# Reordering the attention and first routing stage of a fused attention and two-MoE kernel: loads, fillers, ranks, early products

## The chip, the cores and the metric

The kernel runs on one core of a Trainium2 chip. The metric is the device time of one execution in microseconds (us), lower is better; 485.15 us is the median of three runs of the kernel before (485.13 to 485.38). The engines are named as in the profile: PE (TensorE; PEld is its weight load), DVE (VectorE), ACT (ScalarE), POOL (GpSimd) and SP (SyncE, which here only issues DMAs). Each engine works through its own instructions in order; they wait for one another by semaphores.

## The reference

Three stages follow one another on 2304 tokens (4 batches of 576) of 512 features (8 heads of 64).

```
kv  = einsum('bhsd,bhse->bhde', k, v);  out = einsum('bhsd,bhde->bhse', q, kv)   # linear attention
x   = out / sqrt(mean(out*out, -1) + 1e-6) * g_norm                  # per head
MoE 1:  tokens with x @ w_skip > 0 go to expert argmax(x @ w_gate) of 8:
        x += p_max * (relu(x @ w1[e]) @ w2[e])                       # others pass unchanged
MoE 2:  every token goes to its argmax expert, at most `capacity` tokens per expert (in token order):
        out = p_max * (relu(x @ w1[e]) @ w2[e]), zero for tokens beyond it
```

All inputs and outputs are float32. Which token goes to which expert is known only at run time, so the experts' batches are built on the chip.

## The kernel before, in words

Tokens are worked on as 18 tiles of 128. Everything that this case turns on lies in the first 78 us of 484.

**Attention stage.** SP loads k and v of the four batches (`load_kv`, into the shared weight buffers `wraw`) and q, transposed on the way in as `qT` (`load_q`). Per batch, `emit_kv` multiplies v by k in five chunks c0 to c4 of the sequence, ACT copies the result to `vk`, and `emit_kvT` multiplies it by the gate weights and transposes it; ACT copies both into `kvbd`. Per tile, `emit_products` multiplies q by `kvbd` (one 128x162 product for each of four head pairs: 128 outputs and 34 router logits) into one of three `ops` tiles of PSUM. `emit_tile` then squares on ACT, sums on DVE (`ss`), takes the root on ACT and the reciprocal on DVE (`ri`), scales the logits on DVE (`lh`, then a reduction into `xa`); the outputs go by an ACT copy to `xa`, where POOL multiplies them by the gain `au` and then by `ri`. A finished tile of `xa` is stored by SP to the DRAM table `xcat`.

**Routing.** `rank_part1` makes a one-hot expert matrix `oh` (DVE), counts and ranks by products with ones and triangles (PE, letter R), and builds for each tile a comparison matrix `As` (DVE), which PE multiplies by `Bt` into a table of token numbers by expert (letters E for tiles 0 to 8, T for tiles 9 to 17). It runs twice. The first pass covers tiles 0 to 8: it finds the expert with most tokens (`lead1`), a register is loaded with its number (`order_1l`), SP loads its weights, and POOL gathers its first 128 tokens from `xcat`. These 128 tokens are slot 0's early rows; their transposes (letter q), first-layer products h0 to h3 (`l1`) and second-layer products y0 to y3 (`l2`) are PE work that needs no second pass. The second pass covers tiles 9 to 17 after the last tile. `sort_experts` orders the experts by count, `by_slot` sorts the table into slots, and `rests` sums what exceeds the slots' capacities to one number `nrest`. All engines load `nrest` and branch on it (`If(nrest > 0)`); for these inputs the branch is not taken, but nothing behind it starts before. Behind it stands the rest of MoE 1 and all of MoE 2, beginning with `t1`, PE transposes of gathered rows.

**What sets the order.** PE's order is written by hand: `ATT_SEQ` has one string per batch (t = a tile, c = a chunk of the next batch's k-v product, T = `emit_kvT`, r/R = a rank pass on DVE / on PE, e/E = register / early table, m = products alone, g = gain alone, s = store, w = one weight load, f = fillers, q, h as above), and `EARLY_SEQ` what follows the attention. `WARM_0`, `WARM_T`, `WARM_E` are counts of filler products (of zeros, nobody reads them) on PE. The other engines are ordered by a scheduler, with `behind(a, b)` to keep a behind b.

Of the kernel before, what the change touches and what calls it, by code (L numbers as in the profile page):

```python
# [18 lines left out]
T = B * S  # L19
# [21 lines left out]
WARM_E = 12  # L41
# [7 lines left out]
def moe_kernel(ctx: ExitStack, tc: tile.TileContext, qT, kk, vv, aux, w1a, w2a, w1b, w2b, capacity, out):  # L49
# [68 lines left out]
    cap_i = cst.tile([128, 2], I32, name="cap_i")  # L118
    nc.scalar.dma_start(out=cap_i, in_=capacity.bitcast(I32).unsqueeze(0).to_broadcast([128, 2]))
    capf = cst.tile([128, 1], F32, name="capf")  # L120
# [93 lines left out]
    def rank_part1(st, i0, i1, bump=None):  # L214
# [33 lines left out]
        if prev is not None:  # L248
            counts()
            key = rt.tile([128, E], F32, name="key_1")  # L250
            nc.vector.tensor_tensor(out=key, in0=cps, in1=st["head"], op=ALU.add)
            cnt0 = rt.tile([1, E], F32, name="cnt0_1")
            after = nc.vector.tensor_copy(out=cnt0, in_=cps[0:1])
            st.update(ends=cnt0)
            sort_experts(st, key)
# [13 lines left out]
        row, lead = (lg[:, 256:384], lead1(lg, cps, ranked, st)) if prev is None else (rowb, iter(()))  # L269
# [25 lines left out]
    def lead1_rest(lg, cps, st):  # L295

        order, key, mx = st["lead"]
        lack, oneP = (lg[:, c:c + E] for c in (228, 236))
        one = rt.tile([128, E], F32, name="lead_1l")
        nc.vector.tensor_scalar(out=one, in0=key, scalar1=mx, scalar2=None, op0=ALU.is_equal)  # L300
        nc.vector.tensor_scalar(out=oneP, in0=key, scalar1=mx, scalar2=None, op0=ALU.is_equal)
# [5 lines left out]
        st["lead"] = order, one, bump, head  # L307
# [23 lines left out]
    def sort_experts(st, key):  # L331
# [3 lines left out]
        v.tensor_tensor(out=G, in0=key.unsqueeze(1).to_broadcast([128, E, E]),  # L335
                        in1=key.unsqueeze(2).to_broadcast([128, E, E]), op=ALU.is_gt)
# [109 lines left out]
    def overflow(m, r, w1, w2, gcol0, limit, add_tokens):  # L446
# [4 lines left out]
        with tc.If(nrest > 0):  # L451
            with tc.tile_pool(name=nm("ov"), bufs=1) as ov, tc.tile_pool(name=nm("ovp"), bufs=1, space=PSUM) as ovp:
# [214 lines left out]
    def l1(j, fp, c0=0, c1=None, early=False):  # L667
# [4 lines left out]
        hp = p1h.tile([128, 2, c1 - c0], F32, name="hp1")  # L672
        for ff in range(2):
            fc = fp * 2 + ff
            wv = W[j][fc // 4].rearrange("p (f k m) -> p f k m", f=4, k=4)
            for k in range(4):
                nc.tensor.matmul(hp[:, ff, :], lhsT=wv[:, fc % 4, k, :], rhs=XT[j][:, k, c0:c1], start=(k == 0), stop=(k == 3))  # L677
        if j in SPLIT1:
# [43 lines left out]
    with att:  # L722
        warm(p1u.tile([128, 512], F32, name="acc"), 10)
# [34 lines left out]
        for b in range(B):  # L758
            load_kv(b)
            load_q(b)  # L760
# [24 lines left out]
        def emit_kvT(b):  # L785

            vk, kb = vk_all[b % 2], kvbd_all[b % 2]
            if b == B - 1:
                spare.append(apo.tile([128, 4, 256], F32, name="ops").rearrange("p c n -> p (c n)"))
                tp = spare[0][:, 0:512].rearrange("p (c n) -> p c n", c=4)  # L790
# [3 lines left out]
            wp = p1u.tile([128, 4, 128], F32, name="acc")  # L794
# [37 lines left out]
        def emit_gain(i):  # L832

            gained.add(i)
# [4 lines left out]
            else:  # L839
                nc.scalar.copy(out=og4, in_=o4)  # L840
                multiply(og, og, grep.unsqueeze(1))

        def emit_tile(i):
# [9 lines left out]
            if i not in gained:  # L853
                emit_gain(i)
# [13 lines left out]
        with tc.manual_schedule(engines={mybir.EngineType.PE}):  # L868
            emit_kv(0, range(5))
            emit_kvT(0)  # L870
            def early1():

                order, one, bump, r1["head"] = r1["lead"]
                ahead["reg"] = slot_reg(order, 0, False)
                W[0] = []
                return one, bump

            def early1_rows(n, one):
# [3 lines left out]
                for i in range(n):  # L882
# [650 lines left out]
```

## Time and profile before

| | |
|---|---|
| median of 3 runs | 485.15 us |
| profiled execution, device time | 485.83 us |
| its span (first to last instruction) | 484.1 us |
| PE busy | 470.4 us, 97% of the span |
| DVE, ACT, POOL busy | 298.8, 203.6, 145.3 us |
| moved by DMA | 104.90 MB in 23641 packets |

A line of the timeline gives the start in us from the beginning of the span, the length in us, engine, source line of the kernel before, operation, tiles written and read, shapes and the count of instructions merged into the line; in brackets the idle time of the engine just before it and what released it. The profiled execution lies 1.73 us above its own span; that part is outside the first and last instruction. PE is the busiest engine by far, but its gaps are not spread evenly: most lie in the first 78 us.

### The profile page before, as it was taken

The numbers are of one execution on the slowest core, as the hardware profiler recorded it, in microseconds if no ns is written. First come the engines' busy times: TensorE is split into PE (matmuls) and PEld (weight loads), VectorE is DVE, ScalarE is ACT, GpSimd is POOL, SyncE is SP. The second block draws the span as 40 slices with busy tenths as digits, with TensorE's granted clock in tenths as the row PEclk, the third lists the DMA queues.
The fourth block names the chain that finished last, engine by engine and source line by source line (L and its number), as shares of the span: only waits on it lengthen the run. The fifth ranks groups of instructions, "written<-read, shape, count | busy, mean of one in ns | idle before, by whom it ended". The sixth has DMA issues, their size and how long they took to land.

```text
span 484.1 us, 10279 instructions
## 1 busy us (share of the span) xinstructions
PE 470.4 (97%) x3852; PEld 444.6 (92%) x3852; DVE 298.8 (62%) x950; ACT 203.6 (42%) x507; POOL 145.3 (30%) x179
## 2 busy tenths in 40 slices
PE   8999989999999999999899999999999999999995
PEld 3788788999999999999798999999999999999985
DVE  2367786676676755448694664756747656776611
ACT  1575542545353331225142553554545544555400
POOL 5586865022213113111243220401506033040201
PEclk9999999999999999999999999999999999999999
DMA  7999967997876955566039964554755566310001
GB/s 264 396 395 351 326 227 256 323 367 288 289 238 219 329 195 195 173 231 247 24 94 413 391 259 168 201 189 129 248 176 191 185 229 213 110 38 1 36 24 40
DMA packets 23641, 104.90 MB, mean 217 GB/s; under 512 B 3529, under 2 KB 3657, under 8 KB 14880
## 3 DMA queue, kind: packets, MB, share of 16 engines
q1 hardware_dynamic: 16144, 76.70, 44.6%
q0 software_dynamic: 7152, 27.40, 16.2%
q8 instruction: 32, 0.52, 0.4%
q14 instruction: 25, 0.20, 0.1%
q10 hardware_dynamic: 288, 0.07, 0.1%
HBM read 92.15 MB, written 12.76 MB: 217 GB/s over the span
## 4 chain that ended last, share of the span: by engine, by line
PE 74%; DVE 5%; DMA 3%; issue 1%; ACT 0%; POOL 0%; POOLq 0%; ACTq 0%
PE hp L677 13%; PE yp L1197 8%; PE yp L1198 8%; PE yp L1199 8%; PE hp L1197 6%; PE yp L701 6%; PE hp L1198 6%; PE hp L1199 6%; PE yp L711 3%; PE yp L702 2%; PE yt L1426 2%; PE tp L1382 2%; DMA wraw<-in_w2b 1%; DVE wlo L1087 1%; PE tp L659 1%; PE tp L1118 1%
## 5 line engine op out<-in xcount | busy, mean ns | idle before, releaser
L1086 ACT CAST whi<-wraw 128x512 fp32r<-128x512 f32 x152 | 86.3, 621 | 75.2 <-PE yp L1198 30.1
L1087 DVE TENSOR_TENSOR wlo<-wraw,whi 128x512 fp32r<-128x512 f32 x152 | 97.4, 684 | 28.9 <-ACT whi L1086 27.7
L416 POOL DMA_INDIRECT rows<-xcat,gi x40 | 42.6, 1064 | 149.0 <-ACT ex L425 87.8
L1197 PE MATMUL hp<-xh,whi 128*128 128x256 f32 (+7 forms) x256 | 78.9, 308 | 0.3 <-DVE hl L1217 0.2
L1199 PE MATMUL hp<-xh,wlo 128*128 128x256 f32 (+7 forms) x256 | 76.7, 299 | 0.0
L1198 PE MATMUL hp<-xl,whi 128*128 128x256 f32 (+7 forms) x256 | 76.6, 299 | 0.0
L677 PE MATMUL hp<-xT,wraw 128*128 128x140 f32 (+8 forms) x560 | 75.6, 291 | 0.5 <-ACT xT L661 0.5
L677 PEld LDWEIGHTS hp<-xT,wraw 128*128 128x128 f32 x560 | 71.6, 190 | 2.6 <-issue 1.8
L1197 PE MATMUL yp<-hh,whi 128*128 128x320 f32 (+5 forms) x192 | 58.8, 306 | 0.0
L1416 POOL DMA_INDIRECT out<-ot,toki x24 | 32.9, 1372 | 83.3 <-DVE su L429 39.5
L1198 PE MATMUL yp<-hl,whi 128*128 128x320 f32 (+5 forms) x192 | 57.3, 298 | 0.0
L1199 PE MATMUL yp<-hh,wlo 128*128 128x320 f32 (+5 forms) x192 | 57.3, 298 | 0.0
L1197 PEld LDWEIGHTS hp<-xh,whi 128*128 128x128 f32 x256 | 48.2, 188 | 1.0 <-DVE hl L1217 0.7
L1198 PEld LDWEIGHTS hp<-xl,whi 128*128 128x128 f32 x256 | 48.4, 189 | 0.0
L1199 PEld LDWEIGHTS hp<-xh,wlo 128*128 128x128 f32 x256 | 48.3, 189 | 0.0
L701 PE MATMUL yp<-hT,whi 128*128 128x352 f32 (+4 forms) x160 | 43.1, 351 | 0.0
L1136 POOL DMA_INDIRECT xcat<-rows,toki x16 | 17.0, 1062 | 82.4 <-DVE mxt L374 79.9
L1216 ACT ACTIVATE hh<-hp 128x320 fp32r<-128x320 f32 (+8 forms) x64 | 27.2, 430 | 32.2 <-PE hp L1199 27.4
L1217 DVE SCALAR_TENSOR_TENSOR hl<-hp,hh 128x320 fp32r<-128x320 f32 (+8 forms) x64 | 30.1, 477 | 13.7 <-ACT hh L1216 12.5
L702 PE MATMUL yp<-hT,wlo 128*128 128x176 f32 (+4 forms) x160 | 37.8, 236 | 0.0
L1198 PEld LDWEIGHTS yp<-hl,whi 128*128 128x128 f32 x192 | 36.2, 189 | 0.0
L1197 PEld LDWEIGHTS yp<-hh,whi 128*128 128x128 f32 x192 | 36.1, 188 | 0.0
(284 smaller groups left out, 854.2 us busy)
## 6 DMA issues: line engine op xcount, KB each, us to landing
wraw<-in_w2a SPq DMA_DIRECT2D x14, 1024.0 KB, 6.6
wraw<-in_w1b SPq DMA_DIRECT2D x14, 1024.0 KB
wraw<-in_w2b SPq DMA_DIRECT2D x14, 1024.0 KB, 5.2
wraw<-in_w1a SPq DMA_DIRECT2D x13, 1024.0 KB
xcat<-xa SPq DMA_DIRECT2D x18, 264.0 KB, 5.2
q<-in_q SPq DMA_DIRECT2D x4, 1152.0 KB
wraw<-in_k SPq DMA_DIRECT2D x6, 512.0 KB, 9.6
wraw<-in_v SPq DMA_DIRECT2D x6, 512.0 KB
```

Source lines behind the costliest of these rows:

```text
L416: return nc.gpsimd.indirect_dma_start(out=rows[:n], out_offset=None, in_=xcat[0:source], in_offset=bass.IndirectOffsetOnAxis(ap=gi[:n], ax ...
L677: nc.tensor.matmul(hp[:, ff, :], lhsT=wv[:, fc % 4, k, :], rhs=XT[j][:, k, c0:c1], start=(k == 0), stop=(k == 3))
L701: nc.tensor.matmul(yp, lhsT=wh[:, fc, :], rhs=HT[j][:, fc], start=(fc == 0), stop=False, skip_group_check=True)
L702: nc.tensor.matmul(yp[:, 0, :], lhsT=wl[:, fc, :], rhs=HT[j][:, fc, 0, :], start=False, stop=(fc == 7), skip_group_check=True)
L1086: nc.scalar.copy(out=hi[:, cs], in_=raw[:, cs])
L1087: ins = nc.vector.tensor_tensor(out=lo[:, cs], in0=raw[:, cs], in1=hi[:, cs].bitcast(F32), op=ALU.subtract)
L1197: nc.tensor.matmul(ps, lhsT=wh, rhs=xh, start=first, stop=False)
L1198: nc.tensor.matmul(ps, lhsT=wh, rhs=xl, start=False, stop=False)
L1199: nc.tensor.matmul(ps, lhsT=wl, rhs=xh, start=False, stop=last)
L1216: ea = nc.scalar.activation(out=hh[:, fs, cs], in_=hp, func=AF.Relu)
L1217: ev = nc.vector.scalar_tensor_tensor(out=hl[:, fs, cs], in0=hp, scalar=0.0, in1=hh[:, fs, cs].bitcast(F32), op0=ALU.max, op1=ALU.subtract)
L1416: st = nc.gpsimd.indirect_dma_start(out=out, out_offset=bass.IndirectOffsetOnAxis(ap=r2["toki"][:nn, j, bi:bi + 1], axis=0), in_=ot[:nn], ...
```

## The change

1. `load_kv` reads with `(p c) d` in place of `(c p) d`: a partition's two rows of 2 KB lie together, so one packet has 4 KB. Batch 0 is loaded in two halves of 512 KB like the others, not in four steps of 256 KB.
2. `cap_i` is one row of 8 bytes, no longer broadcast to 128 partitions; the place that needs it on all partitions loads it inside a branch that is not taken.
3. Fillers: 14 in place of 10 at the very start; 0, 3, 0, 0, 0 in place of 5, 3, 5, 2, 0 between batch 0's chunks; 6 in place of 12 after the early table (E).
4. The last batch's q is loaded behind the stores of tiles 0 to 8 (letter l). SP then issues all four weight loads of slot 0 ahead of the stores of tiles 9 to 17; before, one came from POOL and two stood between stores.
5. `kvT(2)`, and `kv(3)` and `kvT(3)`, use `ops` tiles in place of `lg` and `acc`, so the first rank pass finds `lg` free.
6. The first rank pass (R) stands on PE ahead of tile 9's products; `As` is compared with the bf16 row `rowb`, not with a copy of it in PSUM (whose product L238 goes); what only the second pass needs of the first (`lead1_bump`) comes after the early table.
7. Tiles 12 and 14 get their gain on DVE from PSUM, without ACT copy and POOL multiplication. The gather is no longer put ahead of POOL's multiplications.
8. The copy of the early rows' transposes goes from DVE to ACT; h0 moves from between the products of tiles 15 and 16 to behind all tiles, and y1 from behind T to ahead of it.
9. `sort_experts` of the second pass is put behind the early slot's tokens, which need T.

```diff
-G_DVE = ()
-EARLY_SEQ = "h1 x h2 R h3 y0 T y1 y2 y3"
-ATT_SEQ = ["t0 c0 c1 t1 t2 c2 c3 c4 t3 T s", "t0 t1 t2 c0 c1 t3 t4 c2 c3 c4 T s", "r c0 c1 t0 R e m1 g1 s9 w c2 c3 c4 m2 T E f p1 p2 t3", "t0 t1 s10 w s11 q t2 h0 t3 t4 s14 w s r"]
-WARM_0 = (5, 3, 5, 2, 0)
+G_DVE = (12, 14)
+EARLY_SEQ = "h0 h1 x h2 R h3 y0 y1 T y2 y3"
+ATT_SEQ = ["t0 t1 c0 c1 t2 c2 c3 c4 t3 T s", "t0 t1 t2 c0 c1 t3 t4 c2 c3 c4 T s l", "r c0 c1 R m0 g0 e m1 g1 c2 c3 c4 E T f p0 p1 w w w w t2 t3", "t0 t1 s9 s10 q t2 t3 s12 t4 s r"]
+WARM_0 = (0, 3, 0, 0, 0)
-WARM_E = 12
+WARM_E = 6
-    cap_i = cst.tile([128, 2], I32, name="cap_i")
-    nc.scalar.dma_start(out=cap_i, in_=capacity.bitcast(I32).unsqueeze(0).to_broadcast([128, 2]))
+    cap_i = cst.tile([1, 2], I32, name="cap_i")
+    nc.scalar.dma_start(out=cap_i, in_=capacity.bitcast(I32).unsqueeze(0))
...
-            nc.tensor.matmul(lg[:, 256:384], lhsT=ones[0:1], rhs=rowb[0:1], start=True, stop=True)
...
-            sort_experts(st, key)
+            st.update(ends=cnt0, key=key)
...
-            ahead["first"] = nc.vector.tensor_scalar(out=As[:, i0 + i, :], in0=row, scalar1=a[:, i:i + 1], scalar2=None, op0=ALU.is_equal)
+            ahead["first"] = nc.vector.tensor_scalar(out=As[:, i0 + i, :], in0=rowb, scalar1=a[:, i:i + 1], scalar2=None, op0=ALU.is_equal)
...
-        warm(p1u.tile([128, 512], F32, name="acc"), 10)
+        warm(p1u.tile([128, 512], F32, name="acc"), 14)
...
-            step = 1 if b == 0 else 2
-            for c in range(0, 4, step):
+            for c in range(0, 4, 2):
                 for t, src in ((k0, kk), (v0, vv)):
-                    nc.sync.dma_start(out=t[:, c:c + step, :], in_=src[b, o:o + 512].rearrange("(c p) d -> p c d", c=4)[:, c:c + step, :])
+                    nc.sync.dma_start(out=t[:, c:c + 2, :], in_=src[b, o:o + 512].rearrange("(p c) d -> p c d", c=4)[:, c:c + 2, :])
...
             load_kv(b)
-            load_q(b)
+            if b < B - 1:
+                load_q(b)
...
-                kvp[b] = p1u.tile([128, 4, 128], F32, name="acc")
+                if b == B - 1:
+                    spare.append(apo.tile([128, 4, 256], F32, name="ops").rearrange("p c n -> p (c n)"))
+                    kvp[b] = spare[-1][:, 0:512].rearrange("p (c n) -> p c n", c=4)
+                else:
+                    kvp[b] = p1u.tile([128, 4, 128], F32, name="acc")
...
-                spare.append(apo.tile([128, 4, 256], F32, name="ops").rearrange("p c n -> p (c n)"))
-                tp = spare[0][:, 0:512].rearrange("p (c n) -> p c n", c=4)
+                wp, tp = (spare[-1][:, o:o + 512].rearrange("p (c n) -> p c n", c=4) for o in (0, 512))
+            elif b == B - 2:
+                tp = apo.tile([128, 4, 256], F32, name="ops").rearrange("p c n -> p (c n)")[:, 0:512].rearrange("p (c n) -> p c n", c=4)
...
-                ahead["gather"] = g
-                W[0].append(load_w(w1a, 1, nc.values_load(r1["lead"][0][0:1, 0:1], engines=[mybir.EngineType.Pool], min_val=0, max_val=E - 1,
-                                                          skip_runtime_bounds_check_because="the index of an expert"), nc.gpsimd, g))
...
+                    elif u == "l":
+                        load_q(B - 1)
...
-                        nc.vector.tensor_copy(out=XT[0][:, :, 0:128], in_=lg.rearrange("p (c n) -> p c n", c=4))
+                        nc.scalar.copy(out=XT[0][:, :, 0:128], in_=lg.rearrange("p (c n) -> p c n", c=4))
...
-                        W[0].append(load_w(w, hf, ahead["reg"], nc.sync, ahead["store"]))
+                        W[0].append(load_w(w, hf, ahead["reg"], nc.sync))
...
                         lead_tokens(r1, ips1.rearrange("p e (q b) -> p e q b", q=2), EQ1, slice(1, 2))
+                        sort_experts(r1, r1["key"], r1["last"])
                         by_slot(r1, ips1, 1, E, r1["last"])
```

Three places show what the text means for the engines. First PE, from tile 14's products to the branch, in the kernel before; L821, L933, L677, L711, L963 are a tile's products, q, l1 (h0, h1, ...), l2 (y0, ...) and T in the kernel before. Of T's nine products one stands.

```order
L821 MATMUL ops<-kvbd_198,q_249 128x162 x4
L933 MATMUL lg<-ident,rows 128x128 x4
...
L677 MATMUL lg<-xT_918,wraw 128x128 x8
L821 MATMUL ops<-kvbd_198,q_249 128x162 x8
L677 MATMUL hp_1024<-xT_918,wraw 128x128 x8
L677 MATMUL hp_1035<-xT_918,wraw 128x128 x8
...
L677 MATMUL hp_1094<-xT_918,wraw 128x128 x8
L711 MATMUL yp_1105<-hT_943,wraw 128x128 x8
...
L963 MATMUL acc<-Bt_202,As 128x32
L711 MATMUL yp_1105<-hT_943,wraw 128x128 x8
L711 MATMUL yp_1144<-hT_943,wraw 128x128 x16
...
L451 COMPARE_AND_BRANCH
```

The same place in the changed kernel, where the lines are L835, L947, L683, L719, L977 and L459:

```order
L947 MATMUL lg<-ident,rows 128x128 x4
L835 MATMUL ops<-kvbd_202,q_618 128x162 x12
L683 MATMUL hp_987<-xT_891,wraw 128x128 x8
L683 MATMUL hp_997<-xT_891,wraw 128x128 x8
L683 MATMUL hp_1008<-xT_891,wraw 128x128 x8
...
L683 MATMUL hp_1055<-xT_891,wraw 128x128 x8
L719 MATMUL yp_1066<-hT_986,wraw 128x128 x16
...
L977 MATMUL acc<-Bt_206,As 128x32
L719 MATMUL yp_1117<-hT_986,wraw 128x128 x16
...
L459 COMPARE_AND_BRANCH
```

h0 has moved behind the last tile's products, and half of the y products now stand ahead of T, half between T and the branch (before: a quarter and three quarters).

Second DVE, from the sum of the second pass's one-hot to the branch, in the kernel before; `G`, `slot`, `EQ`, `oe`, `of`, `order` are the sort's six instructions.

```order
L251 TENSOR_TENSOR key_1059<-lg,head_1l 128x8
...
L335 TENSOR_TENSOR G_1063<-key_1059 128x64
...
L338 TENSOR_REDUCE slot_1065<-G_1063 128x8
...
L340 TENSOR_TENSOR EQ_1067<-rowf,slot_1065 128x64
...
L328 CAST order_1073<-of_1071 1x8
...
L271 TENSOR_SCALAR As<-rowb,a_9_1079 128x128 x7
L621 TENSOR_TENSOR lt_1_1123<-acc,lead_1l 128x16
...
L350 TENSOR_SCALAR toki_205<-tok_204 128x1
L358 TENSOR_TENSOR T_1_1_1129<-acc,EQ_1067 128x224
...
L396 CAST nrest_1229<-nrf_1227 1x1
...
L451 COMPARE_AND_BRANCH
```

And in the changed kernel:

```order
L250 TENSOR_TENSOR key_1032<-lg,head_1l 128x8
...
L269 TENSOR_SCALAR As<-rowb,a_9_1040 128x128 x7
L633 TENSOR_TENSOR lt_1_1093<-acc,lead_1l 128x16
...
L356 TENSOR_SCALAR toki_209<-tok_208 128x1
L339 TENSOR_TENSOR G_1099<-key_1032 128x64
L344 TENSOR_REDUCE slot_1101<-G_1099 128x8
L346 TENSOR_TENSOR EQ_1103<-rowf,slot_1101 128x64
L328 TENSOR_TENSOR oe_1105<-EQ_1103,rowf 1x64
L364 TENSOR_TENSOR T_1_1_1111<-acc,EQ_1103 128x224
...
L402 CAST nrest_1202<-nrf_1200 1x1
...
L459 COMPARE_AND_BRANCH
```

The sort has moved from ahead of `As` (which T needs) to behind `lt` and `toki` (which need T), between T and `nrest`.

Third SP, from the early expert's register to the branch, of the changed kernel; L762 is the last q, L407 the register, L412 the weight loads, L961 stores.

```order
L961 DMA xcat<-xa 128x528 [waits DVE_49,DMAHW2_49,Activation_49,Pool_49]
L762 DMA q_618<-in_q 128x2304 [waits DMAHW3_49,PE_49]
L407 TENSOR_LOAD order_1l [waits DVE_49]
...
L412 DMA wraw<-in_w1a 128x2048 [waits DMAHW4_49]
...
L412 DMA wraw<-in_w1a 128x2048 [waits DMAHW5_49]
...
L412 DMA wraw<-in_w2a 128x2048 [waits DMAHW6_49,PE_49]
...
L412 DMA wraw<-in_w2a 128x2048 [waits DMAHW7_49]
L961 DMA xcat<-xa 128x528 [waits DVE_49,DMAHW0_49,Activation_49,Pool_49]
```

Before, q's load stood ahead of all stores, the register behind ten stores, and one w1a and two w2a loads lay among the stores of tiles 10 to 17; now four loads of 1 MB are issued in a row.

## Rows read from the trace of the kernel before

**Rows 1.** Windows: busy us (instructions) per engine, granted clock, DMA share, GB/s.
```profile
0.00:6.20 6.20, 4.23 (x10) 1.36 (x11) 1.19 (x7) 1.49 (x2) 2.40 (x29) 1.00 0.52 126
...
48.00:56.00 8.00, 7.71 (x49) 5.44 (x49) 5.33 (x22) 3.46 (x9) 6.20 (x6) 1.00 0.89 281
...
91.00:484.00 393.00, 385.59 (x2985) 373.42 (x2983) 242.92 (x712) 164.70 (x413) 88.14 (x78) 1.00 0.55 193
```
**Rows 2.** DMA from 0 to 80 us: share and GB/s by 2 us; one issue.
```profile
DMA  0959999999999999999999786998998996600669
GB/s 2 260 96 384 406 438 386 388 387 417 400 388 385 388 427 397 381 386 420 398 378 385 282 305 159 381 303 281 379 397 339 267 315 271 260 7 8 156 175 255
...
cap_i<-in_capacity ACTq DMA_DIRECT2D x1, 1.0 KB
```
**Rows 3.** Timeline from 0 to 17 us.
```profile
1.37 0.39 ACTq L119 DMA_DIRECT2D cap_i<-in_capacity  x1
...
1.48 4.23 PE L112 MATMUL acc<-zb 128*128 128x512 bf16 x10 [1.48 <-DVE zb L107]
...
6.21 0.69 PE L777 MATMUL acc<-wraw 128*64 128x64 f32 x16 [0.51 <-DMA wraw<-in_v]
6.80 0.15 DVE L121 CAST capf<-cap_i 128x1 f32<-128x1 int32 x1 [1.92 <-DMA cap_i<-in_capacity]
...
6.83 1.25 PE L112 MATMUL lg<-zb 128*128 128x512 bf16 x5
...
8.36 0.69 PE L777 MATMUL acc<-wraw 128*64 128x64 f32 x16 [0.28 <-DMA wraw<-in_v]
...
12.69 0.68 PE L777 MATMUL acc<-k,v 64*64 64x64 f32 x16
```
**Rows 4.** Timeline from 36 to 60 us.
```profile
39.20 0.24 DVE L159 TENSOR_REDUCE lg<-xa 128x9 f32<-128x72 f32 x1 [1.76 <-ACT kvbd L804]
...
47.60 0.54 PE L883 MATMUL acc<-Bt,As 128*128 128x32 bf16 x9
...
48.38 2.75 PE L112 MATMUL ops<-zb 128*128 128x512 bf16 x12 [0.24 <-ACT kvbd L804]
...
49.80 1.28 POOL L416 DMA_INDIRECT rows<-xcat,gi  x1 [4.24 <-DMA xcat<-xa]
...
51.19 4.53 PE L821 MATMUL ops<-kvbd,q 128*128 128x162 f32 x32
...
55.56 0.60 PE L933 MATMUL lg<-ident,rows 128*128 128x128 f32 x4
...
56.26 0.68 DVE L934 COPY xT<-lg 128x512 f32<-128x512 f32 x1
...
57.67 1.95 PE L677 MATMUL lg<-xT,wraw 128*128 128x128 f32 x16
```
**Rows 5.** Timeline from 59 to 79 us.
```profile
61.67 3.73 PE L677 MATMUL hp<-xT,wraw 128*128 128x128 f32 x32
...
66.73 0.42 PE L241 MATMUL lg<-oh,ones 128*128 128x72 bf16 x9 [1.33 <-DVE oh L167]
...
67.53 0.57 DVE L335 TENSOR_TENSOR G<-key 128x64 f32<-128x64 f32 x1
...
68.17 0.20 DVE L338 TENSOR_REDUCE slot<-G 128x8 f32<-128x64 f32 x1
...
70.81 0.72 PE L963 MATMUL acc<-Bt,As 128*128 128x32 bf16 x9
...
71.38 5.60 PE L711 MATMUL yp<-hT,wraw 128*128 128x128 f32 x48
...
74.85 0.14 DVE L396 CAST nrest<-nrf 1x1 int32<-1x1 f32 x1
...
76.45 0.23 DVE L422 TENSOR_REDUCE nx<-rows 128x1 f32<-128x8 f32 x2 [1.45 <-DVEq L451]
...
77.52 0.63 PE L659 MATMUL tp<-ident,rows 128*128 128x128 f32 x4 [0.45 <-PEq L451]
```

More of the change, by code (lines that the diff above doesn't have):

```diff
@@ L297, in lead1_rest, with lead1_bump @@
         order, key, mx = st["lead"]
-        lack, oneP = (lg[:, c:c + E] for c in (228, 236))
         one = rt.tile([128, E], F32, name="lead_1l")
         nc.vector.tensor_scalar(out=one, in0=key, scalar1=mx, scalar2=None, op0=ALU.is_equal)
+        st["lead"] = order, one, lg, cps, key, mx
+    def lead1_bump(st):
+        order, one, lg, cps, key, mx = st["lead"]
+        lack, oneP = (lg[:, c:c + E] for c in (228, 236))
         nc.vector.tensor_scalar(out=oneP, in0=key, scalar1=mx, scalar2=None, op0=ALU.is_equal)
@@ L306, in lead1_rest @@
         nc.vector.scalar_tensor_tensor(out=head, in0=oneP, scalar=8192.0, in1=sev, op0=ALU.mult, op1=ALU.add)
-        st["lead"] = order, one, bump, head
+        st["head"] = head
+        return bump
     def run(gen):
@@ L329, in first, with sort_experts @@
         return order
-    def sort_experts(st, key):
+    def sort_experts(st, key, after=None):
         m = st["m"]
@@ L334, in sort_experts @@
         G = rt.tile([128, E, E], F32, name=f"G_{m}")
-        v.tensor_tensor(out=G, in0=key.unsqueeze(1).to_broadcast([128, E, E]),
-                        in1=key.unsqueeze(2).to_broadcast([128, E, E]), op=ALU.is_gt)
+        ins = v.tensor_tensor(out=G, in0=key.unsqueeze(1).to_broadcast([128, E, E]),
+                              in1=key.unsqueeze(2).to_broadcast([128, E, E]), op=ALU.is_gt)
+        if after is not None:
+            behind(ins, after)
         slot = rt.tile([128, E], F32, name=f"slot_{m}")
@@ L408, in load_w @@
             behind(ins, after)
+        if note is not None:
+            note["gather"] = ins
         return t
@@ L671, in l1 @@
             HT[j] = m1.tile([128, 8, 2, n], F32R, name="hT1") if j in SPLIT1 else m1.tile([128, 8, n], F32, name="hT1")
-        hp = p1h.tile([128, 2, c1 - c0], F32, name="hp1")
-        for ff in range(2):
+        if 0 in ffs:
+            YP["hp"] = p1h.tile([128, 2, c1 - c0], F32, name="hp1")
+        hp = YP["hp"]
+        for ff in ffs:
             fc = fp * 2 + ff
@@ L677, in l1 @@
                 nc.tensor.matmul(hp[:, ff, :], lhsT=wv[:, fc % 4, k, :], rhs=XT[j][:, k, c0:c1], start=(k == 0), stop=(k == 3))
+        if 1 not in ffs:
+            return
         if j in SPLIT1:
@@ L793, in emit_kvT @@
             warm(tp, WARM_T)
-            wp = p1u.tile([128, 4, 128], F32, name="acc")
+            if b < B - 1:
+                wp = p1u.tile([128, 4, 128], F32, name="acc")
             for hp in range(4):
@@ L830, in multiply, with emit_gain @@
                 behind(ins, ahead["gather"])
-        def emit_gain(i):
-            gained.add(i)
+        def emit_gain(i, whole=True):
             og = xa[:, i, 0:D].rearrange("p (h d) -> p h d", h=H)
@@ L838, in emit_gain @@
                 nc.vector.tensor_tensor(out=og4, in0=o4, in1=grep.unsqueeze(1).unsqueeze(1).to_broadcast([128, 4, 2, HD]), op=ALU.mult)
-            else:
+                return
+            if i not in gained:
                 nc.scalar.copy(out=og4, in_=o4)
+            gained.add(i)
+            if whole:
                 multiply(og, og, grep.unsqueeze(1))
@@ L871, in early1 @@
             def early1():
-                order, one, bump, r1["head"] = r1["lead"]
+                order, one = r1["lead"][0:2]
                 ahead["reg"] = slot_reg(order, 0, False)
                 W[0] = []
-                return one, bump
+                return one
             def early1_rows(n, one):
@@ L951, in moe_kernel @@
             att.close()
-            with tc.tile_pool(name="e1h", bufs=2, space=PSUM, reuse_waits="tile") as p1h, \
-                    tc.tile_pool(name="e1y", bufs=2, space=PSUM, reuse_waits="tile") as p1y:
+            with tc.tile_pool(name="e1y", bufs=2, space=PSUM, reuse_waits="tile") as p1y, \
+                    tc.tile_pool(name="e1h", bufs=2, space=PSUM, reuse_waits="tile") as p1h:
                 for u in EARLY_SEQ.split():
```

39 lines of the change are left out of this document (18 added, 21 removed).

## The prediction

> **What bounds the kernel now.** I read the busy time by windows first. From 91 to 484 us PE is busy for 385.59 of 393 us [rows 1]: what is left there, 7.4 us, is a few short waits and the last store. The change touches nothing in it. So the time is the moment at which PE comes past the branch, `t1` at 77.52 [rows 5], plus a constant: a microsecond that this moment moves is a microsecond of the whole. Next I read the start by the DMA's slices and the timeline, because PE's first useful product waits for data, then backwards from `t1`: which instruction was last?
>
> The start: PE waits for v and begins at 6.21; the fifth chunk begins at 12.69 and ends at 13.37 [rows 3]. The DMA engines run at about 390 GB/s in nearly every slice of 2 us, but in that from 4 to 6 us at 96 [rows 2]; in that time one small load is open, `cap_i`, issued at 1.37 and read at 6.80 after a wait of 1.92 [rows 3].
>
> The end of the stage: y1 to y3 stand behind T and end at 71.38 + 5.60 = 76.98; `nrest` is ready at 74.99, and DVE comes out of the branch 1.46 later, at 76.45 [rows 5]. PE is thus the later one by only about half a microsecond; the number that the branch needs is close behind. This is the place on which my forecast turns.
>
> **The change part by part.**
>
> *Start.* With halves of 512 KB, c0 and c1 need 1.05 MB landed. From row to row: 6.2 us at 126 GB/s moved 0.78 MB [rows 1], and c1, whose k and v complete the same 1.05 MB, began at 8.36 [rows 3]. At about 400 GB/s the 1.05 MB are through at 6.9, so some 1.5 us lie between the bytes and the semaphore. All of batch 0 with its odd ends is 2.62 MB: through at about 10.7, seen at 12.2, so c4 would end at 12.9 against 13.37. If only packets and steps change, the gain is 0.5 us. If the dip goes with the 128-fold `cap_i`, then (390 - 96) GB/s x 2 us = 0.59 MB come earlier, or 1.5 us more: 2.0. Fewer fillers are needed for this: before, 5, 3, 5, 2 of about 0.25 us (1.25 for five) stand on PE between the chunks [rows 3] and would hold it. I add an estimated 0.3 for packets of 4 KB, which no row here shows, bounded by 0 and 0.7. I take 2.3; ends 0.5 and 2.7. Fourteen first fillers at 0.42 (4.23 / 10) end at 1.48 + 5.9 = 7.4 if all run at this length; the later ones take 0.25, so they may end at 6.5. Either is about where data lands.
>
> The Trainium skill's "DMA: Bandwidth & Descriptors" (Specifications) asks for at least 512 B per transfer for line rate and says that below it the engine does a read-modify-write. By that rule 2 KB packets were already long enough and the 0.3 is nothing, while `cap_i`, 1.0 KB over 128 partitions, is the case that it warns of; the trace agrees so far as the dip lies under that load. The sum by the rule would be 2.0.
>
> *First ranks.* Batches 0 and 1 pass the shift on, since PE and DMA both run without gaps there. The first one-hot began at 39.20 after 1.76 us behind an ACT copy out of `lg` [rows 4]; with `lg` free that wait goes: 39.20 - 2.3 - 1.76 = 35.1. R comes right behind; without tile 9's sums and roots among the DVE's rank instructions and with a cheaper `As`, I count 4.6 us in place of 6.0 from R to the last `As`: E begins at 41.9, where it began at 47.60 [rows 4]. Of these 5.7 only part arrives: `kvT(3)`, which ran ahead of E, now runs behind it, and `kv(3)` still needs its data and two ACT copies. I place its end at 44.7. Six fillers fewer give 6 x 0.23 = 1.4 [rows 4].
>
> *Tiles 11 to 17.* A tile of products takes 4.53 / 4 = 1.13 on PE, but three PSUM tiles and ACT's two passes pace it at about 1.25. From 46.0, tiles 11 and 12 take 1.2 each; tile 13, which lies over two batches and has twice the products, 1.75; tile 14 waits about 1.0 for the PSUM of tile 11 and takes 1.3: 52.5. q waits about 0.5 for its rows and takes 0.6 [rows 4]; three tiles more, with 0.25 of waiting, end at X = 57.6. Before, X was 61.67 with h0's 1.95 in it [rows 4, 5]. So 4.1 earlier, of which 1.95 is work that is now behind; for equal work 2.1 to 2.2, about the start's shift. The two gains on DVE cost it 2 x 0.68 or so and the q copy gives 0.68 back [rows 4]; POOL loses two multiplications. I cost these at 0: DVE is busy 5.33 of 8 us there [rows 1]. If DVE is not free, each delays one tile's `ss` by 0.7, hidden by PE's remaining h products.
>
> *From X to the branch.* h0, h1, h2 take 3 x 1.87 (3.73 / 2) = 5.6 [rows 5]: 63.2. R needs the last one-hot; before, PE waited 1.33 for it [rows 5]. Now it comes at about the same time as h2 ends; 0.5 for R. h3, y0, y1 take 5.6: T begins at X + 11.7 and ends at X + 12.4. y2, y3 take 3.7, and PE has done all at X + 16.5 = 74.1. That alone would be 76.98 - 74.1 = 2.9 us of gain.
>
> But the sort now stands behind T. Before, T's end to `nrest` was 74.99 - 71.53 = 3.46 with the sort done long before. Now its six instructions are added, one dependent on the next: G 0.57, then 0.20 each as `slot` [rows 5], of which `order` can be hidden: about 1.45. `nrest` = X + 12.4 + 3.46 + 1.45 = X + 17.3 = 74.9. From there 1.46 to the far side of the branch: X + 18.75 = 76.35. What is queued behind that wait is everything: all engines take this branch. PE stands still for about 2 us in front of it. Against 77.52 the gain is 1.2. The profiled execution would be 485.83 - 1.2 = 484.6; it lies 0.7 over the median, so on the median 484.0.
>
> The sort ahead of `As` was not free before, but what it delayed there (up to 1.5 us of T) is hidden now by h3, y0 and y1, which hold PE until 69.3, when `As` is long done.
>
> **The rivals.** *A, the start does not move* (the dip is the first loads' own, not `cap_i`'s). For: share 0.52 in the first 6.2 us may be the ramp. Against: the slice before the dip already moved 260 GB/s [rows 2]. Then the shift is 0.5, X = 59.4, past the branch at 78.15: +0.6, 485.8.
>
> *B, the branch does not bind.* The sort's instructions overlap with others or the branch costs PE less than DVE's 1.46: PE itself shows only 0.45 at `t1` [rows 5]. Then PE's own 74.1 plus filler, branch and 0.45 counts: 74.8, -2.7, 482.4. Against: 3.46 + 1.45 + 1.46 against y2 and y3's 3.7 leaves much to overlap.
>
> *C, slower: the gather comes late.* Four weights of 1 MB are issued in a row at about 42 to 44; at 390 GB/s they hold the DMA engines for 10.6 us, to about 53. The 128 early rows are gathered behind POOL's work on tiles 9 and 10 and share the engines with them; before, the gather was issued at 49.80 and q ran at 55.56 [rows 4]. PE's order is fixed, so q, which stands ahead of tiles 15 to 17, holds them all. The point: if X passes 58.8, that is q begins after 54.2, `t1` is later than before. With q at 55.5, as before, X = 60.1, `t1` at 78.85: +1.3, 486.5. For: the window 48 to 56 is at DMA share 0.89 already [rows 1]. Against: the gather is 0.27 MB on another queue, and it is issued some 1.4 us earlier than before.
>
> *D, the clock falls at the start.* The granted clock is 1.00 throughout [rows 1], but the ten fillers at the start take 0.42 and later ones 0.25 [rows 3], the lower and the upper of 1.2 and 2.4 GHz. With 12 of 15 fillers gone between the chunks, gaps of a microsecond lie between short bursts; chunks, `kvT(0)` and the first tile, about 4 us of work, would double in part, +2: X = 59.6, +0.8, 486.0. The Trainium skill's "TensorE: Matmul & The Clock Gate" (Part 1) tells of an engine that falls back to half rate in each wait for data between thin bursts; no row here shows it fall.
>
> **How the numbers follow.** Forecast 0.52, A 0.14, B 0.16, C 0.13, D 0.05. The forecast's own range is 483.1 to 485.0, from X by 0.6 to either side and 0.3 for the sort. The range to hold 8 of 10 reaches to B and C: 482.0 to 486.5. Faster by over 0.2% (1 us, what a measurement of this kernel can tell) means under 484.2: three fifths of the forecast's case, all of B and a little of A: 0.52. Slower means over 486.1: C, half of D and some of A: 0.19. Within: 0.29.
>
> **What will show it.** The start: c4 ends near 11, not 13.4, and no dip in the slice from 4 to 6. The first one-hot near 35 with no wait for `kvbd`; E near 42. q near 53, the last tile's products to 57.6. Then the new thing: a PE gap of about 2 us in front of the branch, with `nrest` at 74.9 and `t1` at 76.4. I am wrong in the step if y3 ends at the branch without a gap (B), in the start if c4 ends after 12.5 (A, D: by its length one sees which), in the tiles if PE waits at q (C).

## The result: 491.85 us, 6.7 slower, and the profile after

| | before | after |
|---|---|---|
| median of 4 runs | 485.14 us | 491.85 us (490.78 to 492.27) |
| ratio, 95% interval | | 1.0134 [1.0117, 1.0152] |
| profiled execution, its span | 485.83, 484.1 us | 490.78, 489.1 us |

The profiled execution of after is the quickest of its four, that of before lies 0.7 us above its median; so the two timelines below account for 5.0 us (489.1 - 484.1) of the 6.7. The forecast was 484.0 us, with 482.0 to 486.5 as its range; it went the wrong way. A run more than 1.5% above the fastest of its kernel counts as slow, and the ratios and ranges here leave such runs out.

First PE's timeline from 40 to 62 us of the changed kernel (L898 is E, L810 and L812 `kvT(3)`, L112 fillers, L835 products of tiles, L947 q).

```profile
43.10 0.24 PE L898 MATMUL acc<-Bt,As 128*128 128x32 bf16 x3
43.50 1.34 PE L898 MATMUL acc<-Bt,As 128*128 128x32 bf16 x6 [0.16 <-DVE As L269]
44.68 0.38 PE L112 MATMUL ops<-zb 128*128 128x512 bf16 x1
45.11 0.97 PE L810 MATMUL ops<-gw,vk 128*128 128x34 f32 x8
45.92 0.64 PE L812 MATMUL ops<-ident,vk 128*128 128x128 f32 x4
46.39 2.69 PE L112 MATMUL lg<-zb 128*128 128x512 bf16 x6
48.87 4.73 PE L835 MATMUL ops<-kvbd,q 128*128 128x162 f32 x32
54.17 1.34 PE L835 MATMUL ops<-kvbd,q 128*128 128x162 f32 x8 [0.57 <-DVE ri L873]
58.66 1.12 PE L947 MATMUL lg<-ident,rows 128*128 128x128 f32 x4 [3.14 <-DMA rows<-xcat,gi]
59.56 2.91 PE L835 MATMUL ops<-kvbd,q 128*128 128x162 f32 x10
```

q, at 55.56 before [rows 4], begins at 58.66, behind the longest wait that PE has in the changed kernel: 3.14 us for the gathered rows. Up to there it was ahead: E began at 43.10 (before 47.60), but tile 14's products ended at 55.51, only 0.2 before those of before (55.72), since PE ran at a granted clock of 0.57 from 46 to 50 us. What stands behind q then runs at half speed: q itself takes 1.12 us (before 0.60).

The issues that lead there, of POOL and of SP in the changed kernel:

```profile
48.00 2.04 POOL L842 TENSOR_TENSOR xa<-xa,ri 128x512 f32<-128x512 f32 x2 [4.61 <-DVE ri L873]
50.21 1.28 POOL L424 DMA_INDIRECT rows<-xcat,gi  x1 [0.17 <-issue]
```

```profile
40.11 0.38 SPq L762 DMA_DIRECT2D q<-in_q  x1
44.97 1.39 SPq L412 DMA_DIRECT2D wraw<-in_w1a  x2
46.62 1.05 SPq L412 DMA_DIRECT2D wraw<-in_w2a  x2
```

The token numbers are ready at 46.28 (`toki` on DVE: 46.13 and 0.15), but POOL first waits 4.61 us for the roots of tile 9 and multiplies twice; so the gather is issued at 50.21, behind 4 MB of weights (issued from 44.97 on) and 1.2 MB of q (issued at 40.11). Its rows are there at about 58.6: 8.4 us later, and from 50 to 56 us the DMA engines are busy throughout (share 1.00, 392 GB/s). The windows of the changed kernel show what the wait did to the clock (columns as in [rows 1]):

```profile
46.00:50.00 4.00, 4.00 (x16) 2.55 (x16) 2.79 (x11) 1.21 (x4) 2.00 (x2) 0.57 0.97 328
50.00:56.00 6.00, 4.94 (x37) 4.23 (x35) 3.84 (x10) 3.62 (x8) 5.00 (x6) 1.00 1.00 392
56.00:64.00 8.00, 5.34 (x23) 5.35 (x24) 3.40 (x10) 2.58 (x8) 3.63 (x4) 0.57 0.74 265
64.00:77.00 13.00, 13.00 (x133) 12.98 (x132) 8.86 (x38) 5.89 (x13) 6.16 (x8) 1.00 0.23 86
77.00:84.00 7.00, 4.64 (x40) 4.18 (x39) 5.24 (x34) 1.37 (x5) 4.40 (x6) 1.00 0.47 116
84.00:88.00 4.00, 4.00 (x24) 4.00 (x23) 2.26 (x11) 0.36 (x1) 1.93 (x2) 0.57 0.91 327
```

The granted clock is 0.57 in three stretches (mostly the lower level, 1.2 GHz), each behind a stretch in which PE stood or stuttered: the nine products of E, the wait at q, the gap at the branch. From the branch on (timeline of after, 60 to 90 us; L240 is R, L977 T, L683 h, L719 y):

```profile
64.82 5.52 PE L683 MATMUL hp<-xT,wraw 128*128 128x128 f32 x48
...
70.18 0.41 PE L240 MATMUL lg<-oh,ones 128*128 128x72 bf16 x9
...
76.03 0.38 PE L977 MATMUL acc<-Bt,As 128*128 128x32 bf16 x9
...
76.26 3.82 PE L719 MATMUL yp<-hT,wraw 128*128 128x128 f32 x32
...
80.62 0.14 DVE L402 CAST nrest<-nrf 1x1 int32<-1x1 f32 x1
...
82.30 0.63 PE L663 MATMUL tp<-ident,rows 128*128 128x128 f32 x4 [2.14 <-DVEq L459]
...
83.15 5.45 PE L683 MATMUL hp<-xT,wraw 128*128 128x112 f32 x32 [0.22 <-ACT xT L665]
```

Against [rows 5] the loss adds up from q on: q 3.10 later; q to R 0.35 longer (11.52 against 11.17); R to T 1.77 longer (y1 stands between); T to `nrest` 0.55 longer; `nrest` to `t1` 0.99 shorter, since before PE was still busy then: `t1` at 82.30 against 77.52, 4.78. Behind it the 32 h products of slot 0 take 5.45 us; where the clock stays up they take 3.83 (below). PE's y products of slot 0 begin at 93.11 against 86.95, 6.2 later.

### The profile page after: what moved, and what is told of

Read it like the earlier page. It is cut to its first block, busy times and chain, and to the rows that moved or that the text cites. A ratio compares the mean times of both kernels' runs of the same rounds, so it can differ in the third digit from the quotient of the medians.

```text
span 489.1 us, 10224 instructions
## 1 busy us (share of the span) xinstructions
PE 471.2 (96%) x3833; PEld 448.3 (92%) x3837; DVE 299.9 (61%) x951; ACT 203.0 (42%) x506; POOL 143.1 (29%) x176
## 4 chain that ended last, share of the span: by engine, by line
PE 80%; DVE 2%; POOL 0%; ACT 0%; issue 0%; POOLq 0%
PE hp L683 14%; PE yp L1212 8%; PE yp L1214 8%; PE yp L1213 8%; PE hp L1212 7%; PE hp L1214 7%; PE hp L1213 7%; PE yp L709 6%; PE yp L719 5%; PE yp L710 2%; PE tp L1397 2%; PE yt L1441 2%; PE tp L1133 1%; PE hp L1279 1%; PE tp L663 1%; PE lg L1120 1%
## 5 line engine op out<-in xcount | busy, mean ns | idle before, releaser
L683 PE MATMUL hp<-xT,wraw 128*128 128x128 f32 (+8 forms) x576 | 79.0, 295 | 0.2 <-ACT xT L665 0.2
L683 PEld LDWEIGHTS hp<-xT,wraw 128*128 128x128 f32 x576 | 75.0, 194 | 2.3 <-issue 1.8
L1431 POOL DMA_INDIRECT out<-ot,toki x24 | 34.5, 1439 | 83.4 <-DVE su L437 39.5
L1213 PEld LDWEIGHTS hp<-xl,whi 128*128 128x128 f32 x256 | 48.4, 189 | 0.0
```

The lines of the kernel that those rows point to most:

```text
L1213: nc.tensor.matmul(ps, lhsT=wh, rhs=xl, start=False, stop=False)
L1431: st = nc.gpsimd.indirect_dma_start(out=out, out_offset=bass.IndirectOffsetOnAxis(ap=r2["toki"][:nn, j, bi:bi + 1], axis=0), in_=ot[:nn], ...
```

## The experiments

They ran on other chips than the first result, where the times of both kernels spread more (the kernel before from 483.2 to 490.4 us); so each is read by its ratio to the runs of before beside it and by its trace.

**The base, again.** The changed kernel unaltered. 

> The changed kernel itself, unaltered, as the base of the two runs with fillers on the same chip. On the first chip it took 490.78 to 492.27 us, 6.7 over the kernel before. I expect 489 to 492, the rows to land about 8 us after the gather, half speed in 46 to 50, 56 to 64 and 84 to 88 us.


Measured: 489.88 us, ratio 1.0098 [1.0058, 1.0138]. q waited 4.01 us for rows that came 7.6 us after the gather; half speed in parts of 56 to 64 and behind the branch, not in 46 to 50. The wait repeats; where the clock falls differs between executions.

```profile
57.84 1.12 PE L947 MATMUL lg<-ident,rows 128*128 128x128 f32 x4 [4.01 <-DMA rows<-xcat,gi]
```

**The gather ahead on POOL.**
```diff
-            if "gather" in ahead:
+            if root and "gather" in ahead:
...
-            multiply(og, og, ri.unsqueeze(2))
+            multiply(og, og, ri.unsqueeze(2), True)
...
+                ahead["gather"] = g
```
Only the multiplications by `ri` are thus kept behind the gather.


> The changed kernel, with the gather of the early rows put ahead of POOL's multiplications by ri of tiles 9 and 10 again (those by the gain stay ahead of it). In the changed kernel the token numbers are ready at 46.3 us, the gather runs at 50.21 and PE's q begins at 58.66 after an idle time of 3.14. Theory P (POOL's order makes the rows late): the gather runs at about 46.5, the rows are there 4 us after it, q begins behind tile 14's products at about 55.5 without a wait, the clock does not fall between 56 and 64 us, and 3.1 us of waiting and some 2.5 us of half speed go: 486 us. Theory W (four weights of 1 MB that are in the DMA queues from 45 us on make the rows late): the rows still need 7 us or more, q begins at 54 to 57 and 1 to 5 us go: 487 to 491. Theory Q (the wait for the rows is not what costs): q comes early and the time stays at 491 to 492.


Measured: 484.92 us, 0.9999 [0.9972, 1.0026]: by the ratios 4.8 us less than the base and level with the kernel before. POOL's gather, then PE, of this run:

```profile
46.51 1.28 POOL L424 DMA_INDIRECT rows<-xcat,gi  x1 [3.13 <-DVE toki L907]
```

```profile
52.48 1.34 PE L835 MATMUL ops<-kvbd,q 128*128 128x162 f32 x8 [0.57 <-DVE ri L873]
55.09 0.66 PE L948 MATMUL lg<-ident,rows 128*128 128x128 f32 x4 [1.27 <-DMA rows<-xcat,gi]
55.59 3.48 PE L835 MATMUL ops<-kvbd,q 128*128 128x162 f32 x24
...
76.91 0.71 PE L663 MATMUL tp<-ident,rows 128*128 128x128 f32 x4 [2.14 <-ACT base L1084]
77.76 5.24 PE L683 MATMUL hp<-xT,wraw 128*128 128x112 f32 x32
```

The gather was issued at 46.51, and q runs at full speed 3.6 us earlier. Theory P holds for the time, theory W for the landing (P had 4 us and no wait at q): the rows still needed 8.5 us (one issue of this run, KB not shown, us to landing last):

```profile
rows<-xcat,gi POOLq DMA_INDIRECT x1, 8.5
```

**The w2a loads later.** 
```diff
-... f p0 p1 w w w w t2 t3", "t0 t1 s9 s10 q t2 t3 s12 t4 s r"
+... f p0 p1 w w t2 t3", "t0 t1 s9 s10 q t2 t3 s12 w w t4 s r"
```


> The changed kernel, with the two w2a loads issued behind the store of tile 12 and not right behind the two w1a loads; POOL's order stays as changed, so the gather runs at about 50.2. Theory W: with 2 MB less in the queues the rows land 4 to 5 us after the gather, q begins at about 55.5 and the clock stays up there: 486 to 487 us. Theory P: the gather's late issue decides, the rows land 6 us or more after it, q begins after 57: 490 us or more.


Measured: 488.47 us, 1.0055 [1.0011, 1.0098], spread from 483.87 to 489.73; the base's interval reaches into this one, so a gain is likely but not shown. The trace (of an execution of 485.97 us) is clear: gather at 50.55, landing

```profile
rows<-xcat,gi POOLq DMA_INDIRECT x1, 5.7
```

and q at 56.30 after 0.73 of waiting:

```profile
56.30 0.65 PE L947 MATMUL lg<-ident,rows 128*128 128x128 f32 x4 [0.73 <-DMA rows<-xcat,gi]
...
78.12 0.63 PE L663 MATMUL tp<-ident,rows 128*128 128x128 f32 x4 [2.14 <-ACT base L1083]
78.97 3.83 PE L683 MATMUL hp<-xT,wraw 128*128 128x112 f32 x32 [0.21 <-ACT xT L665]
```

So both theories hold a part: POOL's order put the issue 3.7 us back, and with the two w2a loads behind the gather it landed 2 to 3 us sooner (5.7 against 8.4 in after and 7.6 in the base). The gap at the branch is 2.14 us here as in after, but the clock held behind it (3.83 us for the 32 products). In the kernel before, profiled again, it took 3.7 us from an issue at 49.31; w1a's second half was issued behind the gather there.

**q behind all tiles.** q after `t4` in the last string. 

> The changed kernel, with PE's transposes of the early rows (q) behind the products of tile 17 and not ahead of those of tile 15; gather and weights as changed. If the place of q in PE's fixed order is what turns late rows into a loss, PE works on to about 59.5 without a gap and without low clock, q runs when the rows are there (58.7), and h0 begins at about 61 in place of 64.8: 3.5 to 4 us less, 488 us, whichever of P and W makes the rows late. If the rows were not the cause: no change.


Measured: 486.63 us, 1.0029 [1.0000, 1.0058]; q at 60.35 without a wait, but h0 only at 62.41, behind its own copy (1.46). By the ratios that is 3.3 us less than the base: it is q's place in a fixed order that made late rows costly; last place is not free either.

**That part alone, in the kernel before.** Four weights from SP in a row, none from POOL, gather not put ahead; all else as before.
```diff
-... s9 w c2 c3 c4 m2 T E f p1 p2 t3", "t0 t1 s10 w s11 q t2 h0 t3 t4 s14 w s r"
+... s9 c2 c3 c4 m2 T E f p1 p2 w w w w t3", "t0 t1 s10 s11 q t2 h0 t3 t4 s14 s r"
...
-                ahead["gather"] = g
...
```


> The kernel before, with one part of the change alone: SP issues the four weight loads of slot 0 in a row (POOL none), and the gather of the early rows is no longer put ahead of POOL's multiplications. Everything else, the start, the rank passes, h0's place, the sort and the fillers among it, is as before. If this part is what made the change slower, the gather moves from 49.8 to about 53 us, the rows land about 8 us after it, PE's q waits until 59 or later in place of 55.5, and the kernel is 3 to 5 us slower than before, 488 to 490 us, with a fall of the clock behind the wait. If the loss needs the earlier tiles of the changed kernel as well (PE arrives at q earlier there), it is 0 to 1 us.


Measured: 492.84 us, 1.0148 [1.0089, 1.0208]: this part alone costs as much as the whole change, and more than the 3 to 5 us expected (7.1). Its PE (L930 is q):

```profile
51.61 4.53 PE L821 MATMUL ops<-kvbd,q 128*128 128x162 f32 x32
61.67 1.12 PE L930 MATMUL lg<-ident,rows 128*128 128x128 f32 x4 [5.53 <-DMA rows<-xcat,gi]
62.58 2.37 PE L821 MATMUL ops<-kvbd,q 128*128 128x162 f32 x8
...
84.88 0.63 PE L659 MATMUL tp<-ident,rows 128*128 128x128 f32 x4 [0.50 <-PEq L451]
```

The gather at 53.37, the rows 8.3 us later, the clock down behind (a tile's eight products take 2.37, not 1.34), `t1` at 84.88.

**The sort ahead of T.**
The first line stands in the second rank pass, the second behind the early slot's tokens.
```diff
+            sort_experts(st, key)
...
-                        sort_experts(r1, r1["key"], r1["last"])
```


> The changed kernel, with the sort of the experts back in the second rank pass, ahead of T. In the changed kernel PE has a gap of 2.14 us in front of the branch, and its clock is at half speed from 84 to 87.8 us. My theory: nrest comes 1.3 to 1.5 us earlier, the gap shrinks to about 0.7, and if that is too short for the clock to fall, 1.9 us more come back: 488.5 us; with the clock still falling 490.3. Rival: the sort delays the As matrices and T by as much as it gives back (As end at 74, T runs at 76.0, so there are 2 us of room): 491.8.


Measured: 487.62 us, 1.0058 [1.0029, 1.0088]: by the ratios 1.9 us under the base, but the two intervals overlap, so by the times this gain is likely and not shown. In the trace PE's gap is 1.29 (0.7 was expected), and behind it the clock holds (3.83 us for 32 products, against 5.18 in the base):

```profile
80.42 0.63 PE L664 MATMUL tp<-ident,rows 128*128 128x128 f32 x4 [1.29 <-PEq L460]
81.27 3.83 PE L684 MATMUL hp<-xT,wraw 128*128 128x112 f32 x32 [0.22 <-ACT xT L666]
```

**What the clock alone costs.** 14 fillers ahead of q; 8 fillers behind y3. 

> The changed kernel, with 14 filler products (0.22 us each at full speed, 3.1 us in all) on PE between tile 14's products and q. They fill the wait for the rows and change nothing else: q cannot run before the rows land at about 58.6. Theory: two thirds of what the late rows cost are not the 3.1 us of waiting but that PE's clock falls to half speed in it and stays there for some 5 us of tiles 15 to 17 and h0 (10 products of tile 15 and 16 took 2.91 us where 12 take 1.68 at full speed): 2 to 2.5 us less than the changed kernel on the same chip. Rival (the clock falls all the same, fillers or not, or costs nothing there): no change, or longer by what the fillers overrun.

 

> The changed kernel, with 8 filler products behind y3, 1.8 us, in PE's gap ahead of the branch. nrest is what the branch waits for, so t1 cannot come earlier; PE's idle time falls from 2.14 to about 1.3 us (the branch's own 1.5 less what overlaps). Theory: the clock stays at full speed behind the branch (with an idle time of 1.29 in the run with the sort ahead of T it did), which gives back 1.4 to 1.9 us (32 products of slot 0 in 3.83 us and not in 5.3 to 5.5) in the runs in which it fell. Rival: no change, or the fillers delay PE's own load of nrest: up to 0.5 us slower.


Measured: 489.15 us, 1.0091 [1.0061, 1.0122], and 489.31 us, 1.0089 [1.0057, 1.0122]: against the base's 1.0098 neither can be told from no change. In the traces both did their work: with the first, the window from 56 to 64 has clock 1.00 and tiles 15 to 17 take 3.48 us in place of 4.61, but PE then waits 0.93 for ACT, so that R follows 10.3 us after q in place of 11.2. With the second, PE's idle time is 0.45 and the 32 products take 3.83, while `t1` stays at 81.34. My two thirds for the clock were wrong: at q it is about 0.9 us, and the wait is the larger part.

**The start.** The capacity to 128 partitions again; packets of 2 KB again. 

> The changed kernel, with the broadcast of the capacity to 128 partitions restored (nothing else of the start). In the changed kernel the fifth chunk begins at 11.55 us, in the kernel before at 12.69, where the DMA engines moved 96 GB/s between 4 and 6 us; in the changed kernel it is 253 there. If the 128 rows of 8 bytes made the dip: it returns, and the fifth chunk begins at 12.3 to 13. If the dip came from the four steps of 256 KB and packets of 2 KB: 253 GB/s or so stay and the fifth chunk begins at 11.5.

 

> The changed kernel, with k and v in packets of 2 KB again (order c p), still in halves of 512 KB and with one row of capacity. If packet length decides the start, the fifth chunk begins at 12 us or later and the slice from 4 to 6 us falls below 200 GB/s. If it does not: 11.3 to 11.7, or earlier, since in the changed kernel the 4 KB packets took longer in the first microseconds beside the gain vector's 532-byte packets.


One execution each (489.34 and 490.52 us, nothing to be told from the times). The fifth chunk in after, with 128 rows of capacity, with 2 KB packets:

```profile
11.55 0.68 PE L789 MATMUL acc<-k,v 64*64 64x64 f32 x16 [0.19 <-DMA v<-in_v]
```
```profile
12.21 0.68 PE L789 MATMUL acc<-k,v 64*64 64x64 f32 x16 [0.19 <-DMA v<-in_v]
```
```profile
10.64 0.68 PE L789 MATMUL acc<-k,v 64*64 64x64 f32 x16
```

Compared with after, the broadcast costs 0.66 us, not 1.5, and the longer packets lose 0.91. Ten traces with the changed kernel's start have the fifth chunk between 11.45 and 11.84, and a second one with 2 KB packets (the last version below) has it at 10.89; so both signs are clear, the sizes to some 0.3 us. The dip between 4 and 6 us, 96 GB/s before, did not come back with either part: 227 GB/s with the broadcast, 410 with 2 KB packets (253 in after). Neither part alone made it.

**A better version.** Gather ahead, w2a late, sort ahead of T; then T ahead of y1 as well; then 2 KB packets as well. 

> The changed kernel with three parts undone together: gather ahead of POOL's multiplications, w2a loads behind the store of tile 12, sort ahead of T. If the three costs are separate (rows late by POOL's order 3.6 us, by the weights 2.7, branch gap 0.9 with its fall of the clock 1.4), the rows land at about 52.5, q runs at 53.9 without a wait, PE comes past the branch at 74.3 to 74.8 and stays at full speed: 480.5 to 482 us, 3 to 4 faster than the kernel before. If the start's 1.15 us are all that the change really gains: 484.

 

> The kernel before, unaltered, profiled on the chip of these runs, where its times spread from 483.2 to 488.6 us. The version with three parts undone comes past the branch 2.3 us before the kernel before's profile of the first chip, yet is only 0.7 us faster here. If the kernel before is itself quicker here up to the branch, its t1 stands near 76 and not at 77.52; if t1 is at 77.5 again, the difference lies behind the branch.

 

> The version with three parts undone (gather ahead on POOL, w2a late, sort ahead of T), and T ahead of y1 again, as in the kernel before. The last As should be ready at about 67.9 us, T runs at 68.1 in place of 69.8, nrest comes 1.7 earlier, at 71.9, and PE's own y1 to y3 end at 73.9: PE's gap at the branch (1.3) shrinks to about 0.5, t1 begins at 74.4 and not at 75.23: 0.8 us less, 482.5. Rival: y1 did no harm there, PE was held by the branch's own latency: no change.

 

> The version with the gather ahead, w2a late, the sort and T as before (482.75 us, 2.6 under the kernel before on its chip), with packets of 2 KB for k and v again. In the changed kernel 2 KB packets brought the fifth chunk from 11.55 to 10.64 us. If that gain passes through, t1 begins 0.9 us earlier, at 74.3, and the time is 481.9 us. Rival: the wait for the rows at q (1.2 us there) or the longer loads of later batches eat it: 482.7 or more.


Measured: 483.36 us, 0.9977 [0.9953, 1.0002]; 482.75 us, 0.9944 [0.9916, 0.9972]; 483.31 us, 0.9958 [0.9931, 0.9984]. The first had been put at 480.5 to 482, with `t1` at 74.3 to 74.8; it is not clear of the kernel before. The kernel before, profiled again (one execution, 486.82 us), came past the branch at 77.86, so it is not quicker there. The second is faster than both kernels; the third cannot be told from it, though its `t1` is at 74.67. PE of the second:

```profile
55.05 0.66 PE L949 MATMUL lg<-ident,rows 128*128 128x128 f32 x4 [1.21 <-DMA rows<-xcat,gi]
...
68.81 0.38 PE L979 MATMUL acc<-Bt,As 128*128 128x32 bf16 x9
69.03 5.60 PE L720 MATMUL yp<-hT,wraw 128*128 128x128 f32 x48
...
75.22 0.63 PE L664 MATMUL tp<-ident,rows 128*128 128x128 f32 x4 [0.50 <-ACT yT L724]
76.25 3.83 PE L684 MATMUL hp<-xT,wraw 128*128 128x112 f32 x32 [0.41 <-ACT xT L666]
```

With y1 to y3 behind T the gap at the branch is 0.50; in the first it was 1.30, and `t1` at 75.23 all the same, because there the rows had come 1.0 us earlier. The second had been put at 482.5 us, which it met, and its `t1` at 74.4, which it missed (75.22).

## Why the prediction was wrong

- **The step that failed: "q waits about 0.5 for its rows".** It put the gather at 48.4 (1.4 before the 49.80 of before) and q at 53.0, so a landing of about 4.6 us. The gather ran at 50.21, behind POOL's wait for tile 9's roots, and q at 58.66: of these 5.7 us, 1.8 are the issue and 3.9 the landing, which took 8.4. The mechanism is that of rival C, named with the right place and the right condition, but it had 0.13 and was priced with q at 55.5, "as before". The arguments set against it were wrong: "0.27 MB on another queue", and an issue 1.4 us earlier than before (it was 0.4 later). The landing was 3.7 us behind one weight, and 7.4 to 8.6 behind two or more that were issued shortly before. That alone, in the kernel before, made it 1.5% slower.
- **The rest of the chain held in part by luck.** With q at 58.66 the prediction's own sum gives `t1` at 82.0 (58.66 + 0.6 + 4.0 + 18.75); measured 82.30. But from q to X, the end of the last tile's products, it took 1.7 us longer (6.3 for 4.6, at half speed), and from X on 1.4 shorter. Ahead of q, too, tile 14's products ended at 55.51, not 52.5 (53.83 in the base, where the clock stayed up from 46 to 50 us); behind the wait for the rows that did not show.
- **The start: 2.3 forecast, 1.14 measured** (0.4 to 1.2 over all traces: 12.28 to 12.69 with the start of before, 11.45 to 11.84 with that of after). Of the two terms the capacity's 1.5 was 0.66, and the packets' +0.3 was -0.91: my bounds for them, 0 to 0.7, left out a loss. If the parts add up, 1.4 us of the gain came from what is left, the larger steps and the fewer fillers; the sum had 0.5 for packets and steps and nothing for the fillers, though the fifth chunk of before shows no wait for data behind its fillers [rows 3]. No run separates these two. In the changed kernel the load of `au` also came later, 6.05 against 4.28 us; with 2 KB packets again it came at 4.07.
- **First ranks.** The wait of 1.76 for `lg` went, as said. But R to the last `As` took 5.8 us (38.74 to 44.58; before, read the same way, 6.5), not 4.6; E, put at 41.9, began at 43.10 and stuttered until 44.84.
- **From X to the branch: the gap was right, its sum was not.** A gap of about 2 us was forecast, 2.14 measured; X to `t1` was 18.75 and came to 17.3 (64.98 to 82.30). Both ends of the gap came about 1.4 us early, which left it as it was: T began 0.65 us sooner after X, and the sort lengthened T's end to `nrest` by 0.9 (4.35 against 3.46), not 1.45. For PE's end the sum also slips: 12.4 + 3.7 is 16.1, not 16.5. The sort behind T makes 0.85 of the gap (without it 1.29), y1 ahead of T another 0.8 (with y1 behind T as well 0.50). Left out was that PE's clock can fall in such a gap; here that cost about 1.4 us behind it.
- **The clock (rival D)** did not fall at the start, where I put it: 1.00 in all slices up to 46 us, with 3 fillers in place of 15 between the chunks, and 32 chunk products took 1.15 us there as later. It fell where PE waited for others later. The Trainium skill's "TensorE: Matmul & The Clock Gate" (Part 1) tells of a kernel whose PE falls back to half rate in the waits for data between its bursts; the trace of after agrees at the waits of 3.14 and 2.14 us, and not at those of 0.6 to 1.0 us between the chunks. Nor does each longer wait bring a fall: with the capacity to 128 partitions q waited 2.66 us, and PE ran on at full speed.

```profile
58.69 0.66 PE L947 MATMUL lg<-ident,rows 128*128 128x128 f32 x4 [2.66 <-DMA rows<-xcat,gi]
59.18 3.48 PE L835 MATMUL ops<-kvbd,q 128*128 128x162 f32 x24
```

- **"`t1` plus a constant" held to some 3 us:** from `t1` to the end of the span it took 405.4 to 408.8 us in the 16 traces. That most of PE's gaps lie in the first 78 us, as said ahead of the prediction, is not so: 5.7 of 13.6 us do, and 7.4 lie behind 91 us.

What is open: why the clock fell in 46 to 50 us, and behind waits of 2 us and more, in some executions and not in others, and how the landing time splits between what is queued ahead of the gather and what is issued just behind it. After slot 0's first y product the profiles still differ by up to 3 us, and no run shows why.

## What to carry to other kernels

A small indirect load that PE waits for should go ahead of the bulk loads in time, not only on another queue (no run here put it ahead of all of them; with 1 MB ahead it landed soonest): count the bytes issued in the microseconds before it, and look at what its issuing engine must wait for first. Where PE's order is fixed, price a late operand with all that stands behind it. A wait of 2 us or more on PE can be paid twice, once as a wait and once as half speed behind it.

## What the runs showed of the hardware

- A gather of 128 rows (0.27 MB) landed 3.7 us after its issue with 1 MB issued in the 3 us before it, 5.7 with 2 MB issued 4 to 5.5 us before it, 7.4 to 8.5 with 2 MB issued in the 1.6 us before it, 7.6 to 8.6 with 4 MB issued in the 6 us before it.
- Packets of 4 KB for k and v brought the fifth chunk's products 0.6 to 1.2 us later than packets of 2 KB (11.45 to 11.84 in ten traces, 10.64 and 10.89 in two).
- Behind 13 of PE's 16 waits of 2.0 to 5.5 us (all traces, 2 to 96 us) the granted clock fell, at q for about 0.9 us of loss (compared once), behind the branch for 1.1 to 1.6; behind three (2.04, 2.14, 2.66 us) it stayed at 1.00.
- The branch took 1.45 us on DVE between `nrest` and the next instruction (1.45 or 1.46 in all 16 traces).
